# Block-sparse attention and a gated feed-forward on one core: one rank per piece of work in place of offsets by kind

## The chip, the core and the metric

The kernel runs on one core of a Trainium2 chip. A core has five engines that run side by side, each through its own program in order: TensorE (PE in the profile; its weight loads are PEld), VectorE (DVE), ScalarE (ACT), GpSimd (POOL) and SyncE (SP). They meet through semaphores. DMA transfers are issued by SP and POOL and carried by 16 DMA engines; those that SP issues form one queue (hardware_dynamic in the profile), those that POOL issues another (software_dynamic). The metric is the time of one execution on the device in microseconds (us).

## The reference

Four batches, eight heads, 768 tokens, 64 values a head. The sequence is cut into 24 blocks of 32 tokens. A query block sees its own block and both neighbours, the first and the last block, and three sampled blocks; the first and the last query block see everything. Duplicates among these count once, which is what the mask is for. The attention's output, 3072 tokens by 512, goes through a gated feed-forward.

```python
scores = scale * np.matmul(q, k.transpose(0, 1, 3, 2))
...
scores = np.where(mask, scores, -1000000000.0)
scores = scores - np.max(scores, axis=-1, keepdims=True)
attn = np.exp(scores)
attn = attn / (np.sum(attn, axis=-1, keepdims=True) + 1e-09)
return np.matmul(attn, v).astype(np.float32)
...
gate = 1.0 / (1.0 + np.exp(-(x @ w_gate)))     # 512 -> 1536
val = x @ w_val                                # 512 -> 1536
return (gate * val @ w_out).astype(np.float32) # 1536 -> 512
```

## The kernel before

**Pieces.** The kernel first describes its work as some 1,390 pieces (class `Op`). A piece is a handful of instructions on one engine, or on either of two, with an estimated duration, the pieces it depends on, the buffers it takes and gives back, and a priority `prio`. A planner (`Planner.run`) then lays all pieces out in an estimated time: at each turn it takes the engine that can start soonest, and on it, among the pieces that can start within 0.02 us of the earliest (0.2 us on TensorE), the one with the lowest priority; for a piece with two engines it takes the one that would end it first. The result is one fixed order of instructions on each engine, with buffers assigned. The planner's times are estimates and reach the chip only as that order: on the chip every engine goes through its list and waits where a semaphore makes it wait. An `after` between two pieces binds the planner alone.

**The attention of a batch b** (names as in the code, b is the first figure):

- `ldv`, `ldk`, `ldq`: loads by POOL's queue (L559, L563), float32 in HBM to float16. In batches 1 to 3 `shk`, `shq` (L722) then put K and Q by row; `vsh` (L773, VectorE) does so for V, `scr` (L782) writes these rows to a scratch in HBM, and from there the rows of a query block's window (`w`, L815, V1) and of its sampled blocks (`vg`, L894, three transfers a block, V2) are gathered; `vfl` and `vfc` (L827, L829) fill in the rows of the first and the last block. `ldq` of batch 1 to 3 is issued behind `shk`.
- `trk`, `trq` (L743, L746): K and Q are transposed on TensorE, `evk`, `evq` (L756, L761, L763) copy them to KT and QT. Batch 0 transposes Q in two parts. `kg` (L870, POOL) gathers the sampled blocks of K, `kfl` (L881) the first and the last.
- Eleven steps of two query blocks each, named after the first block: scores `sc` (L914, L921, TensorE), maximum `mx` (L930, VectorE), exponential with row sums `ex` in two halves (L942, ScalarE), reciprocal `rz` (L949), scaling `sl` in two halves (L962, L965), transposes `tp` (L976, TensorE), copy `te` (L982), product with V `pv` (L995, TensorE), copy to the feed-forward's input `xe` (L1011, L1016). In batches 2 and 3 two steps' scores form one piece. Two pairs of PSUM banks (`spool`) hold scores, two banks (`xpool`, `ptpool`) everything else of the attention.
- The first and last query block, which see all keys, go through `dsc`, `dmx`, `dex`, `dsl`, `dtp`, `dte`, `dpv`, `dxe` (L644, L1046 to L1100), one for each pair of heads.

**The feed-forward** has seven groups of tokens: groups 0 and 1 have 256 tokens, the others 512. A group has twelve slices f of the inner dimension; for each a gate piece `pg{g}_{f}` and a value piece, here written `fv{g}_{f}`, of four matmuls (both L1138), then `th` (tanh, L1146) and `h` (L1151). The outputs follow, `py{g}_{t}` (L1173, twelve matmuls), `ys` (L1180, L1182), `st` (the store by SP, L1187). A group's slices can start once all `xe` and `dxe` of its tokens are done and the slice's weights (`wg`, `wv` in four chunks of three slices, L578; `wo`, L586) have landed. Which slice comes when is open.

**Fill.** Where the plan shows TensorE idle in the first 60 us, matmuls on the identity (`fill`, L1207) are put in, 0.23 us each by the plan.

**Priorities before.** Each piece has a due time from its place in the loop (batch, step, stage); `OFFSETS` adds one number for a kind and batch (`evk1`) and one for a third or quarter of its steps (`ex0.d`). `GATES` lets chunks of the weights go after given gathers of batch 0, `LGATE` the loads of the next batch after a gather of this one. `Planner.FETCH` says how long the planner lets the fetch of 256 of TensorE's instructions take, with and without a transfer by POOL's queue under way.

## Time and profile before

| | us |
|---|---|
| times of the runs | 331.94, 333.45, 333.73 |
| median | 333.45 |
| the profiled execution's own time | 333.25 |
| its span | 331.5 |
| TensorE busy | 309.1 |
| VectorE busy | 241.4 |
| ScalarE busy | 219.1 |
| GpSimd busy | 100.9 |

The span goes from the first instruction to the last; 1.75 us of the profiled execution lie around it. The page's second part cuts the span into 40 slices of 8.29 us. A line of groups reads: line, engine, operation, what is written from what, shapes, count, then busy time, mean duration of one in ns, and the idle time before them with what ended it. Matmuls overlap in the pipeline, so a matmul's own duration is longer than its share of TensorE's time; what a piece costs TensorE is read from the starts of pieces that follow each other without a wait.

### The profile page before, as it was taken

What the parts mean: (1) busy time and instruction counts of PE and PEld (TensorE: products, weight loads), DVE (VectorE), ACT (ScalarE), POOL (GpSimd) and SP (SyncE); (2) the same over time, 40 slices, a digit from 0 to 9 for tenths busy, and PEclk for the clock granted to TensorE, in tenths of its full rate; (3) what the DMA queues carried; (4) which work ended last, traced back from release to release, by engine and by line L of the source; (5) the groups of instructions that cost most, each with busy time, mean ns of one, the idle gap of its engine ahead of it and who ended that gap; (6) DMA issues with size and microseconds to landing.
All of it is one profiled execution on the core that took longest, in us unless ns stands there. A gap on an engine that the chain in (4) does not pass through costs nothing.

```text
span 331.5 us, 12349 instructions
## 1 busy us (share of the span) xinstructions
PE 309.1 (93%) x4568; PEld 187.1 (56%) x4568; DVE 241.4 (73%) x542; ACT 219.1 (66%) x650; POOL 100.9 (30%) x332
## 2 busy tenths in 40 slices
PE   6998887998899799999999999999999999999996
PEld 2555566866766356655555655655655665444443
DVE  3399899936887979878898969999996577504310
ACT  1248889854597789766998566679995868423322
POOL 6499642036743632402330427022220010000000
PEclk9999999999999889999999999999999999999999
DMA  7959999979449862235389093531323400020002
GB/s 116 195 186 228 224 226 227 222 184 269 110 69 231 242 136 87 71 96 145 115 159 190 32 223 114 157 96 35 108 72 116 117 11 3 0 97 32 0 34 95
DMA packets 42063, 41.99 MB, mean 127 GB/s; under 512 B 6323, under 2 KB 38196, under 8 KB 42004
## 3 DMA queue, kind: packets, MB, share of 16 engines
q0 software_dynamic: 17376, 16.39, 30.0%
q1 hardware_dynamic: 24628, 24.83, 25.4%
q8 instruction: 36, 0.59, 0.8%
q14 instruction: 23, 0.19, 0.2%
HBM read 45.97 MB, written 9.44 MB: 167 GB/s over the span
## 4 chain that ended last, share of the span: by engine, by line
PE 62%; DVE 13%; DMA 9%; issue 5%; ACT 5%; SPq 3%; POOL 1%; POOLq 0%; DVEq 0%
PE bank L1138 30%; PE bank L1173 13%; DMA V<-scr 5%; PE bank L976 4%; PE bank L995 3%; ACT P L942 3%; DMA out_dram<-YS 2%; SPq L894 2%; PE twin L921 2%; DVE NM L930 2%; DVE V L827 2%; DVE HT L1151 2%; PE twin L1207 2%; DVE P L965 1%; DMA scr<-stg 1%
## 5 line engine op out<-in xcount | busy, mean ns | idle before, releaser
L942 ACT ACTIVATE P<-twin,NM 128x256 f16<-128x256 f32 x176 | 81.5, 484 | 16.0 <-DVE NM L930 15.6
L870 POOL COPY KG<-KT 128x64 f32 x264 | 51.1, 245 | 121.2 <-PE twin L921 121.0
L1138 PE MATMUL bank<-XA,wg 128*128 128x512 f16 (+1 forms) x336 | 77.0, 352 | 2.0 <-DVE HT L1151 1.1
L1138 PE MATMUL bank<-XA,wv 128*128 128x512 f16 (+1 forms) x336 | 76.3, 350 | 2.1 <-ACT TH L1146 1.0
L1151 DVE SCALAR_TENSOR_TENSOR HT<-TH,bank 128x512 f16<-128x512 f32 (+1 forms) x84 | 50.9, 608 | 33.9 <-PE bank L1138 29.4
L1173 PE MATMUL bank<-wo,HT 128*128 128x512 f16 (+1 forms) x300 | 65.0, 371 | 0.0
L1146 ACT ACTIVATE TH<-bank 128x512 f32<-128x512 f32 (+1 forms) x84 | 45.5, 543 | 27.6 <-PE bank L1138 24.8
L930 DVE TENSOR_REDUCE NM<-twin 128x4 f32<-128x1024 f32 x44 | 52.4, 1216 | 0.5 <-PE twin L921 0.2
L1138 PEld LDWEIGHTS <-wv 128*128 128x128 f16 x336 | 31.4, 98 | 28.6 <-issue 4.9
L1173 PEld LDWEIGHTS <-HT 128*128 128x128 f16 x300 | 28.5, 98 | 29.8 <-issue 0.3
L1138 PEld LDWEIGHTS <-wg 128*128 128x128 f16 x336 | 30.1, 98 | 22.9 <-issue 3.1
L942 ACT ACTIVATION_READ_ACCUMULATOR P<-twin,NM 128x1 f32 x176 | 38.0, 216 | 0.0
L965 DVE TENSOR_SCALAR P<-P,ZZ 128x256 f16<-128x256 f16 x138 | 35.6, 318 | 1.5
L995 PEld LDWEIGHTS <-V 128*128 128x128 f16 x704 | 26.0, 98 | 13.7 <-issue 6.2
L1182 ACT ACTIVATE YS<-bank 128x512 f32<-128x512 f32 (+1 forms) x16 | 9.1, 571 | 28.7 <-PE bank L1173 28.7
L976 PEld LDWEIGHTS <-P 128*128 128x128 f16 x352 | 22.3, 98 | 9.4 <-issue 1.8
L995 PE MATMUL bank<-PTS,V 128*128 128x64 f16 x528 | 22.0, 193 | 4.3 <-DVE PTS L982 1.8
L976 PE MATMUL bank<-ident,P 128*128 128x128 f16 x304 | 23.5, 219 | 0.8 <-DVE P L965 0.4
L982 DVE COPY PTS<-bank 128x1024 f16<-128x1024 f16 x23 | 15.7, 681 | 6.0 <-PE bank L976 6.0
L962 ACT ACTIVATE P<-P,ZZ 128x256 f16<-128x256 f16 x38 | 17.1, 503 | 3.0 <-DVE ZZ L949 2.9
L921 PE MATMUL twin<-KG,QT 64*32 64x160 f16 x704 | 19.0, 236 | 0.0
L982 ACT COPY PTS<-bank 128x1024 f16<-128x1024 f16 x15 | 15.2, 1010 | 5.7 <-PE bank L976 5.4
(85 smaller groups left out, 372.4 us busy)
## 6 DMA issues: line engine op xcount, KB each, us to landing
V<-scr SPq DMA_DIRECT2D x264, 32.0 KB, 3.0
out_dram<-YS SPq DMA_DIRECT2D x23, 256.0 KB, 2.1
V<-scr SPq DMA_DIRECT2D x14, 288.0 KB, 3.3
stg<-in_v_dram POOLq DMA_DIRECT2D x4, 768.0 KB, 9.1
stg<-in_k_dram POOLq DMA_DIRECT2D x3, 768.0 KB, 14.2
scr<-stg SPq DMA_DIRECT2D x3, 768.0 KB, 4.4
stg<-in_q_dram POOLq DMA_DIRECT2D x3, 768.0 KB, 7.5
V<-scr SPq DMA_DIRECT2D x6, 384.0 KB, 5.4
```

What stands on the lines that cost most here:

```text
L870: pin(nc.gpsimd.tensor_copy(t[:, :, 1 + n], KW[r][:, :, bass.ds(vals[(i - i0) * 3 + n], BLK // 2)]))
L921: pin(nc.tensor.matmul(t[hh][cs, u, c0:c1], QT[r][rs, p, BLK * i : BLK * i + BLK], src, start=False, stop=True, skip_group_check=True))
L930: pin(nc.vector.tensor_reduce(NM[o.slots[hz][1]][:, 0:4], t, axis=AX.X, op=ALU.max, negate=True))
L942: pin(nc.scalar.activation(pb[:, u, :], t[:, u, :], AF.Exp, bias=NM[z][:, x : x + 1], scale=1.0, accum_out=ZZ[z][:, x : x + 1]))
L965: pin(nc.vector.tensor_scalar(pb[:, u, :], in0=pb[:, u, :], scalar1=ZZ[z][:, 2 * hh + u : 2 * hh + u + 1], scalar2=None, op0=ALU.mult))
L976: pin(nc.tensor.transpose(t[:, c * 128 : c * 128 + 128], pb[:, c * 128 : c * 128 + 128], ident))
L982: pin(copy(o)(PTS[pl.handles[hTS][1]].rearrange("k c q -> k (c q)"), banks[o.slots[hT][1]].bitcast(f16)))
L995: pin(nc.tensor.matmul(t[:, u, p, :], vt[:, ws, p * 128 : p * 128 + 128], pt[:, u, c, :, 32 * p : 32 * p + 32], start=(c == 0), stop=(c == ...
L1138: pin(nc.tensor.matmul(t, wt[:, c, f_ * 128 : f_ * 128 + 128], XT[g][:, c, :], start=(c == 0), stop=(c == 3)))
L1146: pin(nc.scalar.activation(TH[o.slots[ht][1]][:, 0:n], banks[o.slots[hg][1]][:, 0:n], AF.Tanh, bias=0.0, scale=0.5))
L1151: pin(nc.vector.scalar_tensor_tensor(HT[:, f_, hoff : hoff + n], in0=TH[o.slots[ht][1]][:, 0:n], scalar=1.0, in1=banks[o.slots[hv][1]][:, ...
L1173: pin(nc.tensor.matmul(t, HT[:, f_, hoff + tt * 128 : hoff + tt * 128 + 128], wo[:, f_, cols], start=(f_ == 0), stop=(f_ == NF - 1)))
```

## The change

Every piece gets a rank of its own (`RANKS`, one number for each piece in the order in which the code makes them), which takes the place of its due time and offsets. The ranks, the gates and the planner's list of durations were annealed together. The instructions themselves, their shapes and their number stay as they are, but for six more matmuls of `fill` (82 for 76) and for pieces that go to the other of their two engines. `trs` makes the last transposes of K and Q, which give the buffer back, depend on the others, whose order among themselves is now open.

The planner's durations: fetch of TensorE's instructions 7.8 and 3.8 us (7.0 and 3.6), `vg` 1.65 (1.6), `evk` 0.88 and 0.76 (0.85 and 0.7), `vfc` of n units 0.06 + 0.56 n on POOL and 0.12 + 0.44 n on VectorE (0.44 n and 0.3 n), `kg` 0.58 (0.54).

```diff
-GATES = {0: 4, 2: 7, 3: 7, 4: 9, 6: 5, 7: 7, 8: 6}
-LGATE = {1: 10, 2: 11, 3: 2}
-OFFSETS = {
-    "dense1": 0.26, "dense2": 0.10, "dense3": 0.10, "evk0": -0.74, "evk1": -0.80, "evk2": -1.45, "evk3": -0.55,
...
-def kind(o):
...
-def third(o, k):
...
+GATES = {4: 5, 7: 10, 10: 10}
+LGATE = {1: 11, 2: 11, 3: 7}
+RANKS = [
+    95, 31, 147, 27, 14, 3, 1, 20, 17, 18, 13, 9, 24, 24, 0, 28, 39, 11, 71, 36, 51, 358, 33, 345, 32, 344, 41, 130,
...
+]
-    PIECE, FIRST, FETCH = 256, 150, {True: 7.0, False: 3.6}
+    PIECE, FIRST, FETCH = 256, 150, {True: 7.8, False: 3.8}
-    VGATHER = [("SP", 1.6)] * 4
+    VGATHER = [("SP", 1.65)] * 4
+            trs = []
...
-                           deps=(shs[-1:] if b else [ld[x if parts > 1 else p * len(ld) // NP]]) + [c_dma] + kq_users[b - 2],
+                           deps=(shs[-1:] if b else [ld[x if parts > 1 else p * len(ld) // NP]]) + [c_dma] + kq_users[b - 2] + (trs if p == NP - 1 and x == parts - 1 else []),
...
+                    trs.append(tr)
...
-                    res.append(P(f"ev{nm}{b}{p}{x}", ("DVE", "ACT"), (0.85, 0.7) if nm == "k" else (0.06 + 0.0044 * n, 0.17 + 0.0055 * n), f_ev, deps=[tr],
+                    res.append(P(f"ev{nm}{b}{p}{x}", ("DVE", "ACT"), (0.88, 0.76) if nm == "k" else (0.06 + 0.0044 * n, 0.17 + 0.0055 * n), f_ev, deps=[tr],
...
-                filled[x] = P(f"vfc{b}{x}", ("POOL", "DVE"), (0.06 + 0.44 * most[x], 0.12 + 0.3 * most[x]), f_fc, port=True,
+                filled[x] = P(f"vfc{b}{x}", ("POOL", "DVE"), (0.06 + 0.56 * most[x], 0.12 + 0.44 * most[x]), f_fc, port=True,
...
-                kg = P(hkg, "POOL", 0.54, f_kg, deps=[kfl[ks], held["POOL"][part][0]], prio=pr - 1,
+                kg = P(hkg, "POOL", 0.58, f_kg, deps=[kfl[ks], held["POOL"][part][0]], prio=pr - 1,
...
-    for o in pl.ops:
-        k = kind(o)
-        o.prio += OFFSETS.get(k, 0.0) + OFFSETS.get(third(o, k), 0.0)
+    for o, rank in zip(pl.ops, RANKS, strict=True):
+        o.prio = rank
```

What the planner makes of it, by the two programs (both can be built without a chip). TensorE's list has 408 pieces in both; the place of some of them, before and after:

| piece on TensorE | place before | place after |
|---|---|---|
| first slice of group 0 | 52 (`pg0_0`) | 52 (`pg0_7`) |
| `pv0_4`, `pv0_6`, `pv0_8`, `pv0_10` | 27, 32, 37, 47 | 46, 47, 48, 50 |
| `pv0_14` | 62 | 82 |
| first `trk` of batch 1 | 97 | 94 |
| first output of group 0 | 96 | 105 |
| first `trq` of batch 1 | 113 | 109 |
| first `sc` of batch 1 | 120 | 116 |
| `pv1_8`, `pv1_10` | 143, 144 | 146, 147 |
| first `trk` of batch 2 | 152 | 154 |
| first `trk` of batch 3 | 261 | 211 |
| first `sc` of batch 3 | 285 | 290 |
| first output of group 4 | 321 | 318 |
| first slice of group 6 | 379 | 379 |

Before, batch 1's first `trk` stands behind all twelve slices of group 0, one slice of group 1 and the first output of group 0; after, behind eleven slices of group 0, one slice and a gate piece of group 1, and no output. SP's list after: the gathers of batch 0 in the order 11, 9, 4, 5, 8, 10, 6, 7, 16, 12, 17, 13, then `w0_18`, 18, 15, `w0_1`, 3, 1, 2, 14, 19, `w0_20`, 21, `scr1`, 22, 20; before: 4 to 9, `w0_18`, 10 to 13, `w0_1`, 14 to 17, `w0_20`, 18, 19, 2, 3, 1, 22, `scr1`, 20, 21. POOL's list: `memset`, on which the mask waits, stands behind the six first transfers after and ahead of them before; `ldv2` and `ldk2` stand behind `kg1_18` and `kg1_19` after, behind `kg1_14` and `kg1_15` before; between `ldk2` and `shk2` stand six `kg` before and seven after; in batch 3 three `vfc` stand ahead of the `kfl` and `kg`. VectorE's list: `vsh1` at place 80 (88 before).

Pieces that change engine, as counts: `vfc` on VectorE 6 (10 before), on POOL 10 (6); `xe` on VectorE 12 (17), on ScalarE 32 (27); `evk` on VectorE 6 (4), on ScalarE 10 (12); `dte` on VectorE 12 (9), on ScalarE 4 (7); `dxe` on VectorE 6 (8), on ScalarE 10 (8); `kfl` on VectorE 6 (4), on POOL 10 (12); one of three `shq` on VectorE (0); `te`, `sl`, `evq` and `ys` one piece each.

## Prediction

> **What bounds the kernel now.** I read the page's busy times first, then the stretches, the waits, and the timelines of TensorE and GpSimd.

> ```profile
> span 331.5 us, 12349 instructions
> PE 309.1 (93%) x4568; PEld 187.1 (56%) x4568; DVE 241.4 (73%) x542; ACT 219.1 (66%) x650; POOL 100.9 (30%) x332
> ...
> DMA  7959999979449862235389093531323400020002
> ...
> PE 62%; DVE 13%; DMA 9%; issue 5%; ACT 5%; SPq 3%; POOL 1%; POOLq 0%; DVEq 0%
> ```

> TensorE is the bound over the whole, with 93%, and DMA is full up to about 83 us (slices 3 to 9). The stretches, cut where TensorE's list has its milestones, tell where TensorE isn't the bound:

> ```profile
> core 0: us, PE busy (x) PEld busy (x) DVE busy (x) ACT busy (x) POOL busy (x), PEclk, DMA share, GB/s
> 18.20:44.60 26.40, 22.43 (x494) 13.66 (x488) 24.07 (x55) 21.23 (x73) 22.71 (x62) 1.00 1.05 200
> 44.60:72.10 27.50, 23.66 (x423) 18.94 (x421) 22.42 (x62) 21.52 (x68) 5.13 (x15) 1.00 1.14 224
> 72.10:86.80 14.70, 12.44 (x157) 9.56 (x155) 10.27 (x17) 6.52 (x15) 9.24 (x20) 1.00 1.00 219
> 86.80:112.90 26.10, 22.27 (x502) 15.21 (x501) 21.86 (x46) 21.31 (x76) 11.90 (x46) 1.00 0.74 167
> 112.90:146.80 33.90, 33.76 (x485) 20.78 (x486) 29.86 (x77) 26.54 (x72) 11.62 (x34) 0.95 0.42 100
> 195.20:243.30 48.10, 47.22 (x837) 28.42 (x835) 43.60 (x91) 37.03 (x111) 13.47 (x63) 1.00 0.41 110
> ```

> In batch 0 (18.2 to 44.6) VectorE is busy 91% of the time; from 112.9 on TensorE 98% and more. Between, TensorE gets behind. The two places that matter most are the transposes of the next batch's K, which wait for its load:

> ```profile
> 69.15 1.89 POOL L722 COPY stg<-stg 96x2048 f32<-96x2048 f32 x1 [12.28 <-DMA stg<-in_k_dram]
> ...
> 95.71 0.89 POOL L559 DMA_DIRECT2D stg<-in_v_dram  x1
> 96.59 0.78 POOL L563 DMA_DIRECT2D stg<-in_k_dram  x1
> ...
> 110.95 1.89 POOL L722 COPY stg<-stg 96x2048 f32<-96x2048 f32 x1 [2.31 <-DVE PTS L982]
> ```

> ```profile
> 109.69 1.04 PE L1138 MATMUL bank<-XA,wg 128*128 128x512 f16 x4
> 112.90 0.51 PE L743 MATMUL bank<-ident,stg 96*128 96x96 f16 x8 [2.17 <-POOL stg L722]
> ```

> K of batch 1 is down at 69.1 and put in order at 71.0; K of batch 2 is issued at 96.6, down 14.2 us later (110.8), and TensorE stands 2.2 us for it.

> **The measure.** What a piece costs TensorE I read from starts of pieces that follow without a wait:

> ```profile
> 286.57 10.52 PE L1173 MATMUL bank<-wo,HT 128*128 128x512 f16 x48
> 296.93 1.03 PE L1138 MATMUL bank<-XA,wg 128*128 128x512 f16 x4
> 297.80 1.03 PE L1138 MATMUL bank<-XA,wv 128*128 128x512 f16 x4
> ```

> An output is (296.93 - 286.57) / 4 = 2.59, a slice piece 0.865 (0.44 with 256 tokens). In the same way scores 0.50, or 0.89 for two steps, `tp` 0.45, `pv` 0.47, transposes of K or Q 0.34 (0.25 for the smaller part of batch 0's Q), `dsc` 0.45, `dtp` and `dpv` 0.34. 120 and 48 slice pieces, 24 outputs, 24 and 10 scores, 44 `tp` and `pv`, 36 transposes of K and Q and 42 dense pieces make 275.2 us; none goes away. So I follow the lag, time less work done; at TensorE's end (328.2) it is 53.0, and 3.3 us of copy and store come after. The column "after" is worked out below.

> | milestone | before: time, work, lag | after |
> |---|---|---|
> | first slice | 44.6, 14.6, 30.0 | 45.4, 14.3, 31.1 |
> | first `trk`, batch 1 | 72.2, 36.6, 35.6 | 72.5, 33.1, 39.4 |
> | first `sc`, batch 1 | 86.8, 48.1, 38.8 | 86.5, 46.3, 40.2 |
> | first `trk`, batch 2 | 112.9, 68.4, 44.5 | 112.6, 69.3, 43.3 |
> | end | 328.2, 275.2, 53.0 | 325.7, 275.2, 50.5 |

> **The change, part by part.**

> *Durations of the planner, `trs`, gates:* they put no instruction on the chip; 0 by themselves. Their cover is total: TensorE's list already runs the transposes in order. The six more fills (6 x 0.23 = 1.4 us) stand before the first slice, where VectorE sets the time.

> *Start.* `memset` behind six issues of POOL (ending at 6.16) moves the mask (3.61 us on VectorE) from 2.0 to about 6.4 to 10.0; VectorE had nothing before 10.7. 0, with 0.7 us of cover; without it each us would shift batch 0. By the sums of VectorE's list the copy that the first slice waits for (`xe0_10`) comes at 31.5 us of its work instead of 30.7: +0.8, so 45.4. The slice is now f = 7, whose weights land at 44.8 in the trace of before and stand as far forward in POOL's queue as then: no further wait.

> *To batch 1's K.* TensorE now has 33.05 - 14.34 = 18.7 us to do before the first `trk`, VectorE 18.9 (31.5 to 50.4), ScalarE 19.5. `vsh1` comes earlier on VectorE and waits for V, down at 64.35, about 2 us; `pv0_14` moves behind 18 gathers (with the windows 24 portions of 96 KB, which before were down at 60.8). Walking through the list with the rows' durations I reach `trk` at 68 to 69, before K is there; that is the cover of all these stalls, some 3 us. K stands behind the same transfers as before, but `scr1` (768 KB, SP) now goes at 65.4 instead of 68.2, beside K. Loads of K took 4.7 us behind V's landing with 27% of the DMA time in SP's queue (64.4 to 69.1) and 7.4 us with 59% (103.4 to 110.8): K is late by 0 to 2.75 us. I take 1.4, the middle, as `scr1` comes in part of the time. 71.1 + 1.4 = 72.5.

> [...] The 27% and 59% agree that SP's queue takes a share when it has work. [...]

> *To batch 1's scores.* Behind the first `trk` stand 13.3 us of work (before 11.5), both outputs of group 0 among it. `shq1` now stands behind one more `vfc` (1.6 us on POOL) and is done at about 81.5, ahead of the `trq` at 83. 72.5 + 13.3 = 85.8; I add 0.7 for gaps marked "issue", of which before had 0.50 and 0.59 here. 86.5.

> *Batch 1.* ScalarE becomes the limit: from the first exponential (1.9 us behind the scores' start) to `te1_8` its list has 12 `ex` (0.90), 6 `th` (0.35), 4 `te` (0.91) and 2 `xe` (0.75), 18.0 us; two more `ex` and two `xe`, 3.3, to `xe1_10`, for which group 2's first slice waits; then 2.2 of TensorE to `trk`. 86.5 + 1.9 + 18.0 + 3.3 + 2.2 = 111.9, with handovers 112.0. If ScalarE were busy at 89%, the highest share that I saw in a stretch (11.19 of 12.6 in 32 to 44.6), it would be 2.6 more; with 0 and 2.6 as ends I take 0.6, nearer 0, since from 40.6 to 44.2 it ran without a wait where its inputs stood ready. 112.6. K of batch 2 doesn't hold it: `ldk2` goes about 95.3, behind `kg1_19`, which `sc1_14` releases at 92.5, and 14.2 + 1.9 make 111.4. So the wait of 2.2 us goes, and ScalarE is what is late next.

> *After.* The lag grew by 8.5 from here. Clock 0.95 in 112.9 to 146.8 is 1.7 of it, unchanged. Batch 3's `trk` go from place 261 to 211, `shk3` being free some 10 us earlier: 0.97 of waits (193 to 195) go. The two gaps of 0.49 and 0.72 at 210 and 222 may; I take 0.3 of them. 7.2 remains. From 112.9 on VectorE loses work (in all 8 us: four `vfc` at 1.3 to 1.8, five `xe` at 0.85, against two `evk`, three `dte`, one `shq`); ScalarE gains 1.2; worth 0, since TensorE hides both. The `vfc` on POOL ahead of batch 3's `kg` need 5 us behind `pv2_1`; 10.1 us of TensorE's work cover them, and without cover sc3 would be late.

> Sum: 3.3 + 325.7 = 329.0, that is 2.5 less than the span; 333.25 - 2.5 = 330.75 as the profiled execution. It lay 0.2 under the median: **331.0**.

> **Rivals.**

> *ScalarE stays behind (slower).* From batch 1's first exponential (88.4) to `pv1_2` ScalarE has 44.8 us of work. At the 82% that it was busy in 86.8 to 112.9 (21.31 of 26.1) it needs 54.6, and `pv1_2` comes at 143.0 with 93.9 of work done, lag 49.1, where before had 47.1 (142.8, 95.7). If nothing is saved later that is 333.45 + 2.0 = 335.5. Below 85% it is slower than before at all. For it: no stretch shows ScalarE over 90%. Against: its waits there were for VectorE, which loses work.

> *Nothing gained.* K of batch 1 at its late end (1.35 more) and ScalarE at 92% (21.3 / 0.92 is 1.85 of waits for 0.6, 1.25 more): 331.0 + 2.6 = 333.6.

> *Gaps in TensorE's own program go (more gained).* "issue" has 5% of the chain:

> ```profile
> 204.60 1.60 issue
> ...
> 221.76 1.09 issue
> ```

> With 0.40 and 0.35 beside them, 3.4 us behind 195. If these are waits for program packets and the longer allowance spreads the dense pieces, 331.0 - 3.4 = 327.6. Against: TensorE's own gaps there are 1.3 us.

> [...]

> **How the numbers follow.** A measurement here can tell 0.5%, 1.7 us, from no change: 331.8 to 335.1. Forecast (328.9 to 331.8) 0.33; gaps go 0.15; nothing gained 0.19; ScalarE 0.33, which holds other stalls of a new order too. Faster 0.48, same 0.19, slower 0.33. Range: down to the gaps' case with K on time and ScalarE without waits (327.6 - 1.4 - 0.6 = 325.6), up to ScalarE's case with K at its late end and the 0.7 of gaps once more (335.5 + 1.35 + 0.7 = 337.5).

> **What would show it.** First slice at 45 to 46; first `trk` of batch 1 at 71 to 74 behind a wait for POOL's copy, now some 3 us; first scores of batch 1 at 86 to 88; no wait of TensorE for POOL at batch 2's K; ScalarE over 90% busy in 88 to 110; TensorE's end near 325.7. Wrong if K of batch 1 lands after 73, if `trk` is reached late because gathers of batch 0 are, or if ScalarE waits in batch 1.

## The result, and the profile after

The changed kernel takes 337.92 us (median of 16 executions, 335.50 to 339.27), the kernel before 333.31 (16 executions, 331.33 to 337.05): a ratio of 1.0141, with a 95% interval of 1.0117 to 1.0165. The change makes the kernel 1.4% slower. The profiled execution took 335.5 us, the fastest of the sixteen, with a span of 333.7.

These are the parts of the changed kernel's page that answer to those shown of before: the span, the busy times, the DMA's slices, and the shares of the chain.

```profile
span 333.7 us, 12285 instructions
PE 310.8 (93%) x4574; PEld 187.6 (56%) x4574; DVE 239.2 (72%) x523; ACT 219.1 (66%) x664; POOL 104.7 (31%) x337
...
DMA  7969999979569774969340143444214120010002
...
PE 65%; ACT 11%; DVE 10%; DMA 8%; issue 3%; SPq 1%; POOL 1%; DVEq 0%; POOLq 0%
```

Nothing in them explains 4.6 us: the busy times have hardly moved. The stretches of the changed kernel do (columns: stretch, its length, busy time of each engine with the number of instructions in brackets, granted clock, DMA share, GB/s):

```profile
core 0: us, PE busy (x) PEld busy (x) DVE busy (x) ACT busy (x) POOL busy (x), PEclk, DMA share, GB/s
...
44.60:72.10 27.50, 23.18 (x450) 18.86 (x449) 23.02 (x55) 21.74 (x76) 5.99 (x20) 0.94 1.14 228
72.10:86.80 14.70, 13.60 (x174) 9.84 (x171) 11.59 (x18) 7.18 (x18) 6.61 (x17) 1.00 0.84 176
86.80:112.90 26.10, 24.55 (x534) 17.42 (x532) 22.29 (x57) 24.33 (x84) 12.73 (x49) 1.00 0.75 163
112.90:146.80 33.90, 33.90 (x491) 20.76 (x490) 29.20 (x58) 27.15 (x76) 14.84 (x35) 1.00 0.83 165
146.80:195.20 48.40, 42.54 (x609) 24.66 (x608) 35.07 (x71) 29.69 (x89) 9.27 (x38) 0.96 0.42 107
195.20:243.30 48.10, 47.45 (x794) 28.27 (x792) 40.50 (x90) 37.83 (x120) 18.15 (x66) 1.00 0.37 103
```

The one stretch of these that the prediction does not show of before:

```profile
146.80:195.20 48.40, 47.41 (x742) 27.76 (x738) 42.01 (x91) 37.99 (x120) 13.80 (x52) 1.00 0.58 135
```

Batch 1 (86.8 to 112.9) went as forecast: ScalarE is busy 24.33 of 26.1 us, 93%, where it had 82%, and TensorE waits less. TensorE is never idle in 112.9 to 146.8. The loss lies in one row: 146.8 to 195.2, where TensorE is idle for 5.9 us (before 1.0) and its clock falls to 0.96 (before 1.00). DMA has moved too: it is busy 0.83 in 112.9 to 146.8, where before it was 0.42.

Lines of the chain of work that ended last, in that stretch of the changed kernel (start, us, what), and below it the timelines of SP, VectorE and TensorE (start, us, what, and in brackets the idle time before and what ended it):

```profile
146.68 2.59 PE bank L1199 x12
149.27 4.53 DMA V<-scr
153.87 6.00 DMA out_dram<-YS
163.77 2.72 PE bank L1164 x8
```

```profile
146.87 2.30 SPq L920 DMA_DIRECT2D V<-scr  x5
149.27 0.88 SPq L841 DMA_DIRECT2D V<-scr  x2
150.40 3.06 SPq L920 DMA_DIRECT2D V<-scr  x6
153.87 0.38 SPq L1213 DMA_DIRECT2D out_dram<-YS  x1
```

```profile
150.53 2.36 DVE L956 TENSOR_REDUCE NM<-twin 128x4 f32<-128x1024 f32 x2 [0.25 <-PE twin L947]
159.96 0.69 DVE L1206 TENSOR_SCALAR YS<-bank 128x512 f32<-128x512 f32 x1 [7.07 <-DMA out_dram<-YS]
160.57 0.58 DVE L1126 CAST XA<-bank 64x32 f16<-64x32 f32 x4
161.18 0.18 DVE L975 RECIPROCAL ZZ<-ZZ 128x4 f32<-128x4 f32 x1
161.40 0.88 DVE L991 TENSOR_SCALAR P<-P,ZZ 128x256 f16<-128x256 f16 x4
162.19 0.17 DVE L975 RECIPROCAL ZZ<-ZZ 128x4 f32<-128x4 f32 x1
162.39 0.48 DVE L991 TENSOR_SCALAR P<-P,ZZ 128x256 f16<-128x256 f16 x2
```

```profile
162.74 1.04 PE L1002 MATMUL bank<-ident,P 128*128 128x128 f16 x8 [5.02 <-DVE P L991]
163.56 1.91 PE L1164 MATMUL bank<-XA,wg 128*128 128x512 f16 x4
```

This is one stall, and the four views show it from end to end. There are three output buffers, `YS`. The planner gave `ys2_3_0`, the fourth output tile's copy of group 2, the buffer of `ys2_0_0`, since by its estimate the store of that one, `st2_0_0`, was down 2.7 us before the copy starts (149.7 for 152.4); another buffer stood free. On the chip `ys2_0_0` is copied by 146.65. SP issues its store only at 153.87, behind two windows (`w2_11`, `w2_15`, L841) and gathers (L920): it is busy issuing these until 153.46, and what the chain names last is the landing of `w2_11`, 0.3 us later (149.27 and 4.53 us). The store lands 6.0 us after its issue, at 159.9. VectorE stands still for 7.07 us at the copy. Behind it in VectorE's list stand `dxe13` and the reciprocals and scalings `rz2` and `sl2` of two attention steps, whose inputs are there by 155.6. So ScalarE gets no work (idle 156.2 to 162.4), and TensorE waits 5.02 us for the transposes `tp2_12`. In the kernel before the copy `ys2_1_0` waits 0.28 us for the same store, and TensorE does not notice:

```profile
155.17 0.69 DVE L1180 TENSOR_SCALAR YS<-bank 128x512 f32<-128x512 f32 x1 [0.28 <-DMA out_dram<-YS]
```

The lags (time less TensorE work done, in us) of the profiled executions, beside the forecast; the last column is the experiment `e5_store_ahead` below:

| milestone | before | forecast | changed kernel | store ahead |
|---|---|---|---|---|
| first slice | 30.0 | 31.1 | 32.2 (at 46.5) | 31.3 |
| first `trk`, batch 1 | 35.6 | 39.4 | 39.0 (72.1) | 38.1 |
| first `sc`, batch 1 | 38.8 | 40.2 | 40.7 (87.0) | 41.1 |
| first `trk`, batch 2 | 44.5 | 43.3 | 44.0 (113.3) | 44.4 |
| first output of group 2 | 47.4 | | 44.6 (143.3) | 45.0 |
| first `tp2` of 157 to 163 | 47.6 | | 49.9 (162.7) | 45.2 |
| TensorE's end | 53.0 | 50.5 | 55.2 (330.5) | 49.2 |

At the first output of group 2 the changed kernel is 2.8 us ahead of before; 20 us later it is 2.3 behind. Where a loss of TensorE is given below without a line of the profile, it is taken from starts in the same way: the start of a piece, less the start of the piece before it and what that one costs. This is up to 0.2 us more than the idle time in the brackets, and it counts as well what half clock costs, that is, a stretch with a granted clock of 0.50.

### The profile page after: what moved, and what is told of

Same layout as the page of the kernel before. It is cut to its first block, busy times and chain, and to the rows that moved or that the text cites. A ratio compares the mean times of both kernels' runs of the same rounds, so it can differ in the third digit from the quotient of the medians.

```text
span 333.7 us, 12285 instructions
## 1 busy us (share of the span) xinstructions
PE 310.8 (93%) x4574; PEld 187.6 (56%) x4574; DVE 239.2 (72%) x523; ACT 219.1 (66%) x664; POOL 104.7 (31%) x337
## 4 chain that ended last, share of the span: by engine, by line
PE 65%; ACT 11%; DVE 10%; DMA 8%; issue 3%; SPq 1%; POOL 1%; DVEq 0%; POOLq 0%
PE bank L1164 31%; PE bank L1199 14%; ACT P L968 6%; DMA stg<-in_q_dram 4%; PE bank L1021 3%; PE bank L1002 3%; PE twin L947 2%; DVE V L853 2%; DMA out_dram<-YS 2%; DMA FL<-scr 1%; ACT PTS L1008 1%; DMA V<-scr 1%; PE twin L1021 1%; DVE NM L1072 1%; PE twin L1002 1%
## 5 line engine op out<-in xcount | busy, mean ns | idle before, releaser
L968 ACT ACTIVATE P<-twin,NM 128x256 f16<-128x256 f32 x176 | 81.5, 486 | 17.3 <-DVE NM L956 16.2
L896 POOL COPY KG<-KT 128x64 f32 x264 | 50.6, 243 | 117.9 <-PE twin L947 112.4
L1164 PE MATMUL bank<-XA,wv 128*128 128x512 f16 (+1 forms) x332 | 75.5, 352 | 0.0
L1177 DVE SCALAR_TENSOR_TENSOR HT<-TH,bank 128x512 f16<-128x512 f32 (+1 forms) x83 | 50.1, 607 | 33.1 <-PE bank L1164 29.7
L1002 PE MATMUL bank<-ident,P 128*128 128x128 f16 x264 | 20.7, 222 | 8.9 <-DVE P L991 6.3
L855 POOL COPY V<-FL 32x768 f32<-32x768 f32 (+1 forms) x20 | 18.3, 944 | 18.9 <-PE bank L1021 15.7
L988 ACT ACTIVATE P<-P,ZZ 128x256 f16<-128x256 f16 x36 | 16.4, 508 | 8.7 <-DVE ZZ L975 8.7
L1021 PE MATMUL bank<-PTS,V 128*128 128x64 f16 x464 | 19.0, 195 | 0.3 <-DVE XA L1037 0.2
L947 PE MATMUL twin<-KG,QT 64*32 64x160 f16 x704 | 18.7, 235 | 0.0
L1037 ACT CAST XA<-bank 64x256 f16<-64x256 f32 x38 | 13.9, 366 | 5.2 <-PE bank L1021 4.8
## 6 DMA issues: line engine op xcount, KB each, us to landing
stg<-in_k_dram POOLq DMA_DIRECT2D x3, 768.0 KB, 14.3
```

The source lines that it names most:

```text
L855: pin(nc.gpsimd.tensor_copy(dst.bitcast(f32), src.bitcast(f32).broadcast_to([BLK, n, DM // 2])))
L896: pin(nc.gpsimd.tensor_copy(t[:, :, 1 + n], KW[r][:, :, bass.ds(vals[(i - i0) * 3 + n], BLK // 2)]))
L947: pin(nc.tensor.matmul(t[hh][cs, u, c0:c1], QT[r][rs, p, BLK * i : BLK * i + BLK], src, start=False, stop=True, skip_group_check=True))
L968: pin(nc.scalar.activation(pb[:, u, :], t[:, u, :], AF.Exp, bias=NM[z][:, x : x + 1], scale=1.0, accum_out=ZZ[z][:, x : x + 1]))
L1002: pin(nc.tensor.transpose(t[:, c * 128 : c * 128 + 128], pb[:, c * 128 : c * 128 + 128], ident))
L1021: pin(nc.tensor.matmul(t[:, u, p, :], vt[:, ws, p * 128 : p * 128 + 128], pt[:, u, c, :, 32 * p : 32 * p + 32], start=(c == 0), stop=(c == ...
```

## The experiments

All but one (`e7_fetch_back`) add lines behind `order = pl.run()`, so that the plan is the same but for what is named. `behind(p, a, b)` stands for "move a and b directly behind p in the order in which the instructions are emitted":

```python
def behind(place, *names):
    moved = [next(o for o in order if o.name == x) for x in names]
    for o in moved:
        order.remove(o)
    at = next(x for x, o in enumerate(order) if o.name == place) + 1
    order[at:at] = moved
```

**Another buffer.** In the first three only the choice among the output buffers differs.

```diff
+    for o in order:
+        for h, y in (("ys2_3_0", 2), ("ys2_1_0", 0)):
+            if h in o.slots:
+                o.slots[h] = ("ys", y)
```

> Theory (one output buffer): in the changed kernel VectorE stands from 152.9 to 160.0 at ys2_3, because its buffer is that of ys2_0, whose store goes at 153.9 and lands at 159.9; TensorE loses 5.1 us at tp2_12 and some 1.2 more just behind. With the free third buffer for ys2_3 (and that of ys2_0 for ys2_1) the order stays and the wait goes: 5 to 6 us less than the changed kernel, about 332 us against 333.3 before, ratio 0.995; TensorE's wait ahead of tp2_12 under 0.5 us. Rival (gathers and DMA late): the softmax of batch 2 waits for rows of V anyway, so TensorE waits further on: at least 336, ratio 1.008 or more. Second rival (clock): the lower granted clock of this order, 0.98 to 0.99, is the cost: 337, ratio 1.012, whatever the buffer.

Measured: 333.10 us (330.86 to 336.01, 12 executions) against 333.31 of before in the same series, ratio 1.0025 (0.9984 to 1.0066). `tp2_12` starts at 157.6 with no wait, and TensorE's end has lag 50.6. The stall goes with the buffer; 4.8 us of the median come back. But the median only equals that of before. Its own waits show why: now `ys2_1_0` uses the buffer of the late store.

```profile
DVE YS L1206 <- DMA out_dram<-YS: 3.0, 1, 3.0
```

The columns are engine and line, what it waited for, us in total, times, and the longest. It is one wait of 3.0 us on VectorE, until 159.4. TensorE loses 1.18 before `fv3_6`, which by the profile waits for the bank that this copy empties, and 0.69 before `fv3_2`, which waits for a piece `h` that stands behind the copy on VectorE.

All outputs in turn, in the changed kernel and in the kernel before:

```diff
+    turn_of = {}
+    for o in order:
+        for h in o.slots:
+            if h.startswith("ys"):
+                o.slots[h] = ("ys", turn_of.setdefault(h, len(turn_of)) % 3)
```

> All output tiles take the three buffers in turn. Buffer theory: as with the one exchange, 331 to 332.5 us, ratio 0.993 to 0.998, since only group 2 waited for a store; up to 1 us less if later groups waited a little too. Rival (gathers, clock): 336 to 338.

> The same turns in the kernel before. Buffer theory: there three copies waited about 1 us each for a store (155.2, 157.5, 161.6) and TensorE lost at most 0.5 near them: 332.5 to 333.5, ratio 0.997 to 1.000. Rival (the buffers are what ails both orders): 330 or less.

Measured: changed kernel in turn 332.93 (331.27 to 336.07), ratio 1.0015 (0.9975 to 1.0055), lag at the end 51.9; before in turn 332.57 (330.35 to 335.04), ratio 0.998 (0.9944 to 1.0016), lag 53.8. In turn, `ys2_1_0` gets the late store's buffer in the changed kernel as well; it starts at 160.7, 0.1 behind the landing, and TensorE loses 1.38 and 0.69. The first is a little above the 331 to 332.5 expected; before gains nothing that can be told from zero. So the buffer rule as such isn't what matters: what matters is a copy that meets this store.

**The store itself.** A first try moved `st2_0_0` directly behind `ys2_0_0`:

```diff
+    first = next(o for o in order if o.name == "st2_0_0")
+    order.remove(first)
+    order.insert(next(x for x, o in enumerate(order) if o.name == "ys2_0_0") + 1, first)
```

> The buffers stay as planned, but SP issues st2_0 directly behind its copy's place, ahead of w2_11, w2_15 and two gathers. If SP's order makes the store late, it lands by 153.5 and all of the 5 to 6 us come back, 332. If the DMA traffic ahead of it makes it late (3 to 6 us from issue to landing), it lands near 153 to 155 and 3 to 5 us come back, 333 to 335. Rival (gathers, clock): 337.

Measured: 337.05 (331.53 to 338.40, 6 executions); store issued at 153.73, down at 160.32, `tp2_12` at 163.2. This missed its aim: no piece of SP stands between `ys2_0_0` and `st2_0_0` in the order, so the lists of all five engines are as they were, and these are six more executions of the changed kernel. Five took 336.77 to 338.40; one took 331.53, and as its trace was not kept, why is open. What holds the store stands ahead of both. The next one moves that away.

```diff
+    behind("st2_0_0", "vg2_5", "w2_11", "w2_15", "vg2_16", "vg2_14")
```

> The changed kernel with its buffers as they are; SP issues the store of the first output of group 2 (st2_0_0) directly behind vg2_9, ahead of vg2_5, w2_11, w2_15, vg2_16 and vg2_14. Theory A (the store is late because SP comes to it late): it is issued at about 148 instead of 153.9, down by 151.5, and VectorE copies ys2_3_0 at 153 as soon as TensorE has the output. The 5.1 us wait of TensorE at 157.7 goes, and with it the two smaller waits of 1.18 and 0.69 that the kernel with exchanged buffers still had at 158 to 163, which were for the same store. Profiled end of TensorE 324 to 326, median 331 to 333. Theory B (the store is late because the DMA queues are full of batch 3's loads, which the new order issues some 35 us sooner): it needs 6 us from issue to landing wherever it stands, is down at 154, VectorE waits 1 us, and the time is that of the kernel with exchanged buffers, 333.

Measured: **329.70** (328.16 to 330.93, 6 executions) against 333.51 (17 executions), ratio 0.9885 (0.9846 to 0.9923). With one store moved past five of SP's pieces the new order is 1.2% faster than before, and below the 331 to 333 expected. SP, then TensorE, of this kernel:

```profile
147.83 0.38 SPq L1213 DMA_DIRECT2D out_dram<-YS  x1
148.40 1.31 SPq L920 DMA_DIRECT2D V<-scr  x3
```

```profile
158.04 0.62 PE L1002 MATMUL bank<-ident,P 128*128 128x128 f16 x8
158.50 1.03 PE L1164 MATMUL bank<-XA,wg 128*128 128x512 f16 x4
159.37 1.03 PE L1164 MATMUL bank<-XA,wv 128*128 128x512 f16 x4
```

The store is issued 6.0 us sooner, is down after 2.1 us (149.94), and the waits of TensorE before `tp2_12`, `fv3_6` and `fv3_2` are gone. Theory A holds for SP's place. That the store now needs 2.1 instead of 6.0 us to land says that theory B has a part as well: DMA is busy 0.49 in 147.8 to 150.0 here, and 1.05 in 153.87 to 159.86 in the changed kernel.

> The changed kernel, with the load of batch 3's Q (ldq30) issued by GpSimd behind the K blocks kg2_11, at about 158 instead of 149. SP's order and the buffers are as in the changed kernel. Theory A: the store still goes at about 153.9, behind the windows and gathers of batch 2 that SP issues ahead of it, and lands at 157 to 160; VectorE waits 4 to 7 us, and the median is 336 to 338. Theory B: without this load in the queues the store is down 2 to 2.5 us behind its issue, at 156.3; VectorE waits 3.4 us instead of 7.1, TensorE 1 to 2 instead of 5.1, and the median is about 334.5.

```diff
+    behind("kg2_11", "ldq30")
```

Measured: 336.51 (335.46 to 342.50, 8 executions), ratio 1.0094 (1.0060 to 1.0127). With batch 3's load of Q out of the way the same store, issued at 154.11, is down at 157.69, after 3.6 us and not the 6.0 to 7.2 of six profiles with this load beside it; VectorE waits 4.05 us instead of 7.07 and TensorE 2.1 instead of 5.0. So the transfers that the new order brings forward do lengthen the store's way, by 2.4 us against the changed kernel, as theory B has it. The time gains little. In the profiled execution, 2.1 us above the median, Q of batch 3 is now late: it lands at 168.64, VectorE copies it (`shq3`, and `evk320` behind it), TensorE loses 3.5 us before `trq320` (170.87), and the half clock of 169.96 to 176.79 takes more. Both causes add up: SP comes to the store 6 us later than it can, and the store then takes 4 us more than it does at 148.

**The same stall put into the kernel before.**

```diff
+    behind("vg2_12", "st2_0_0")
```

> The kernel before, with the same thing put into it: SP issues the store st2_0_0 behind w2_15 and vg2_12, at about 156.3 instead of 150.8; ys2_1_0 uses the same buffer (0), as in the kernel before. If one copy that waits at the head of VectorE's queue is what cost the changed kernel its time, VectorE stands still from 154.2 until the store is down at 158 to 160.5 (instead of 155.1), ScalarE and TensorE follow it, and the median rises by 3 to 5 us, to 336 to 338. If the loss belonged to the new order as a whole and the wait only stood beside it, VectorE's slack takes up such a wait, and the median stays within 1 us of 333.4.

Measured: 336.36 (335.90 to 339.38, 4 executions) against 332.36 (16 executions), ratio 1.0133 (1.0074 to 1.0193). VectorE of this kernel:

```profile
152.18 1.81 DVE L827 COPY V<-FL 32x1536 f16<-32x1536 f16 x2
157.94 0.69 DVE L1180 TENSOR_SCALAR YS<-bank 128x512 f32<-128x512 f32 x1 [3.95 <-DMA out_dram<-YS]
```

One store, issued 4.8 us later (155.62 for 150.83), makes VectorE wait 3.95 us for 0.28. TensorE waits 2.5 before `tp2_4`, and the half clock of 159.35 to 162.77 costs it 1.4 more before `pv2_4`. The old order loses 4.0 us of the median, nearly the 4.6 of the whole change.

**What stands behind the copy.** Here the copy still waits, but last:

```diff
+    behind("sl2_12_0", "ys2_3_0")
```

> The changed kernel with SP's order and the buffers as they are, and ys2_3_0 moved five places back in VectorE's list, behind sl2_12_0. It still waits for the store (down at about 159.9), but dxe13, rz2_14, sl2_14, rz2_12 and sl2_12 no longer stand behind it. If the loss is what stands behind the copy, tp2_12 starts at 158 instead of 162.7; then pg3_6, which needs the bank that ys2_3_0 empties, waits until 160.7, so of 5.1 us about 2 remain, and the median is 334 to 336. If the bank were what TensorE really waits for, the time stays at 337 to 338.

Measured: 340.08 (339.31 to 343.81, 4 executions), ratio 1.0253 (1.0189 to 1.0317). In this kernel the tile's own store `st2_3_0` stands ahead of its copy, so that one output tile is stored from what the buffer held before and is wrong, and the copy has that store to wait for as well: it comes at 165.9, and `pg3_6`, which needs the bank, stood still for 8 us. Its median therefore says nothing about the question. The first half of the expectation can be read all the same: `tp2_12` started at 158.1, lag 45.3, without a wait. The same with the store moved along:

```diff
+    behind("sl2_12_0", "ys2_3_0", "st2_3_0")
```

> The changed kernel with SP's place for st2_0_0 and the buffers as they are, and ys2_3_0 and its own store st2_3_0 moved behind sl2_12_0 in the lists of VectorE and SP. If the loss is what stands behind the copy on VectorE, tp2_12 starts at 158 (lag 45.3) although the copy still comes only when the store is down, at about 160; then pg3_6, which needs the bank that ys2_3_0 empties, waits until 161, 2 of the 5.1 us, and the median is 334 to 336. If that bank is what the time hangs on, the wait only moves from tp2_12 to pg3_6, the lag at pg3_6 stays at 50 or more, and the median is 337 to 338.

Measured: 335.28 (331.93 to 336.82, 10 executions), ratio 1.0052 (1.0012 to 1.0092), within the 334 to 336 expected. This series ran on another chip, with before at 333.63 (13 executions); by the ratios to before it is 3.0 us better than the changed kernel. VectorE:

```profile
158.24 0.48 DVE L991 TENSOR_SCALAR P<-P,ZZ 128x256 f16<-128x256 f16 x2
159.87 1.29 DVE L1206 TENSOR_SCALAR YS<-bank 128x512 f32<-128x512 f32 x2 [1.15 <-DMA out_dram<-YS]
```

The store lands when it did (159.85), and VectorE waits 1.15 us for it instead of 7.07. In the profiled execution, the fastest of the ten, TensorE loses nothing at `tp2_12`; but it had come to batch 2 late, with lag 46.4, since K of batch 1 landed at 70.25, and that covered the store. By the ratios 3.0 of the 8.5 us between the changed kernel and the one with the store ahead (1.0141, 1.0052 and 0.9885) hang on the pieces behind the copy. The other 5.6 would be the copy itself, through the bank that `pg3_6` needs, as expected in kind; no profile of a middling execution shows it, so that part is argued.

**A part undone, and more moves.**

```diff
-    PIECE, FIRST, FETCH = 256, 150, {True: 7.8, False: 3.8}
+    PIECE, FIRST, FETCH = 256, 150, {True: 7.0, False: 3.6}
```

> One part of the change undone: the planner's allowance for TensorE's program packets is 7.0 and 3.6 again; the ranks and the other durations are the new ones. The planner then gives ys2_3_0 the third buffer and ys2_1_0 (on ScalarE) the first, and 112 pieces of TensorE's list stand elsewhere than in the changed kernel. Theory A: the loss of the changed kernel is the one copy that waits for the store, so this kernel has no wait of over 2 us at 155 to 163, and its time is that of the kernels whose buffers were exchanged, 331.5 to 334.5. Rival: the new ranks make an order that is slower in itself, or the longer allowance is what the new order needs; then TensorE's lag is already larger than 45.5 at batch 2's first transposes of K, or its own gaps marked as issue grow by over 1 us behind 195, and the time stays at 336 or above.

Measured: 351.22 (350.47 to 352.78, 4 executions), ratio 1.0525 (1.0479 to 1.0572). TensorE has no wait of over 0.5 us at 155 to 163, and yet it is the slowest of all: the rival's outcome. The sign that the rival named is there, a lag of 46.4 at batch 2's `trk`, but most of the loss comes later: the lag is 47.5 at 160 and 72.5 at the end. Six losses of TensorE of 0.9 to 1.4 us in a row at 207 to 218, the later ones at half clock (211.98 to 222.22), and more at 260 to 272, stand between the steps of one batch's attention. In the first of these stretches TensorE has 184.0 us of work behind it when batch 3's scores start (changed kernel 170.2, before 164.4), so little is left to put between the steps. The 1,387 ranks fit one list of durations: with another list they give another order, which nobody has tuned. So the parts of this change can't be priced one by one, and what the longer allowance alone is worth stays open.

```diff
+    behind("st2_0_0", "vg2_5", "w2_11", "w2_15", "vg2_16", "vg2_14")
+    behind("kg1_6", "shq1")
+    behind("evq130", "vfc12")
+    behind("sl0_2_1", "sl0_2_0")
```

> The store ahead as in e5_store_ahead, and three moves in batch 0 and 1 at waits of TensorE that the profile of the changed kernel shows: the copy shq1 on GpSimd ahead of vfc13; VectorE's vfc12 behind evq130; VectorE's sl0_2_0 directly behind sl0_2_1, so that it does not run beside GpSimd's shk1 (it took 1.99 us there, against 0.48 for others of its kind). The waits of TensorE before tp0_2 (1.27) and before trq110 (1.22) should go or fall below 0.4. If TensorE's lag at batch 2's first transposes of K falls by the same 2 us, to about 42, the median is 2 us below that of e5_store_ahead, 329 to 331. If ScalarE, 93% busy in batch 1, takes the gain back, that lag stays at 43.5 to 44 and the time is that of e5_store_ahead, 331 to 333.

Measured: 329.62 (328.24 to 331.72, 9 executions), ratio 0.9888 (0.9853 to 0.9924), the time of `e5_store_ahead`. The waits before `tp0_2` and `trq110` are gone; but they are not in `e5_store_ahead` either, where TensorE comes to batch 1 earlier and waits 2.2 us for K's copy, so the moves can claim only the 1.0 us that is lost there before `trq120` and not here. With it the first scores of batch 1 come with lag 40.1 instead of 41.1; at batch 2's `trk` it is 44.5 against 44.4. Between these two milestones the lag grows by 3.3 in nine other profiles of this order, here by 4.4: `vfc12`, moved behind `evq130`, takes 1.3 us on VectorE just ahead of `mx1_4`, and ScalarE's first exponential comes 1.1 us later behind the scores (3.0 for 1.9). The gain was given back there by one of the three moves.

> The kernel with the store ahead (e5_store_ahead), and six fill matmuls of 0.23 us (1.4 us in all) ahead of trk100, where TensorE waits 2.2 us for GpSimd's copy of K. All profiles so far show the granted clock in stretches of 3.41 us, and each stretch in which TensorE was busy for under half of the time is followed by one at half clock (nine such pairs; stretches with 54% or more are not). With the fill the stretch at 68 is busy 0.8 instead of 0.40, so the one after it stays at full clock. If that half clock costs what it takes away, 1.7 us of TensorE at most, the lag at batch 1's scores falls from 41.1 to about 40 and the median is 0.5 to 1.5 us below 329.7. If ScalarE takes it back in batch 1, the clock is 1.00 there and the median stays at 329.2 to 330.2.

```diff
+    behind("st2_0_0", "vg2_5", "w2_11", "w2_15", "vg2_16", "vg2_14")
+    at = next(x for x, o in enumerate(order) if o.name == "trk100")
+    bank = order[at].slots["trk100"][1]
+    def f_wait(o):
+        for x in range(6):
+            pin(nc.tensor.matmul(banks[bank].rearrange("p (x n) -> p x n", n=128), ident, ident.unsqueeze(1).broadcast_to([128, 4, 128]),
+                                 start=True, stop=True, skip_group_check=True))
+    order.insert(at, Op("fillk", "PE", 0.0, f_wait, count=6))
```

Measured: 330.77 (328.61 to 333.47, 12 executions), ratio 0.9941 (0.9906 to 0.9976). The two stretches at K of batch 1, first without the fill (`e5_store_ahead`), then with it:

```profile
67.92:71.33 3.41, 1.36 (x20) 1.04 (x19) 1.43 (x4) 0.50 (x2) 2.14 (x2) 1.00 0.78 262
71.33:74.74 3.41, 3.41 (x28) 2.68 (x26) 0.42 (x1) 1.98 (x3) 0.48 (x1) 0.50 0.72 77
```

```profile
66.97:70.38 3.41, 3.05 (x26) 1.96 (x24) 2.00 (x6) 1.28 (x3) 0.97 (x1) 1.00 0.98 313
70.38:73.80 3.42, 2.44 (x39) 2.30 (x40) 0.42 (x1) 1.87 (x3) 1.64 (x2) 1.00 0.41 57
```

With TensorE busy for 3.05 us instead of 1.36 the clock behind stays at 1.00, and the profiled execution has lag 40.1 at the scores and 48.3 at the end, 0.9 less than without the fill. The median shows no such gain: 0.9941 of before against 0.9885 without the fill, with intervals that overlap. Five of its twelve executions, those with a mean clock of 0.999 or more, took 328.6 to 330.1, the seven others 330.7 to 333.5. Where their clock fell isn't recorded, so the effect is shown for one execution; what it is worth over all of them is not.

## Why the prediction was wrong

The forecast was 331.0 us, with a range up to 337.5; it came out as 337.92.

**The step that failed** is the paragraph "After", and in it the sentence that VectorE's change from 112.9 on is "worth 0, since TensorE hides both". It sums VectorE's work over a stretch of 215 us and does not walk through its list. (The sum was off too: from 112.9 on VectorE's busy time fell by 3.3 us, 155.5 to 152.1, and not by 8.) The lag was to grow by 7.2 from batch 2's `trk` to the end; it grew by 11.2. One wait of 5.02 us and the half clock behind it (TensorE busy 2.92 us at clock 0.50 in 162.24 to 165.65, so 1.5 us of work lost) make 6.5. With the store ahead the growth is 4.8, and 11.2 less 4.8 is 6.4. By the medians the stall costs 8.2 us (337.92 less 329.70); the traced execution was the fastest of its sixteen, and where the others lose the rest no trace shows. The trace of before had the three lines that this step needed: a copy by VectorE that waits for `out_dram<-YS`, a store that SP issues only behind gathers, and transfers of batch 3 that the change moves forward by 36 us (`ldv3` and `ldk3` from 167 to 131). The plan of the changed kernel shows the shared buffer and the five pieces ahead of the store. The prediction listed places on TensorE and POOL, and of SP's list only batch 0.

**Start.** Forecast 45.4 with lag 31.1, measured 46.5. The profiled execution ran a half-clock stretch at 18.9; the seven profiles of this order that have none there show 45.3 to 46.0, lag 31.0 to 31.6. Right but for that stretch. The cover of the mask was larger than written: only its last four instructions wait for `memset` (1.64 us), and it ends at 7.0, not at 10.0.

**Batch 1's K.** The 1.4 us for `scr1` beside it were not there: K landed at 68.97, with `scr1` issued at 66.4. In ten profiles of this order (not counting `e7_fetch_back`) it landed at 68.9 to 69.4, but for one at 70.25; in three of the old order at 69.0 to 69.9. That K comes late when SP's queue takes a larger share of the DMA time was an estimate from two loads of before, and it did not show: in 64.4 to 69.0 SP's queue had 59.8% of the DMA time (before 25.8%), and the moved bytes rose from 181 to 292 GB/s, so K paid nothing. The milestone came right, 72.1 for 72.5, by luck: TensorE itself arrived there 3 us late, through the late start, a half-clock stretch at 56.4 and a loss of 1.40 before `tp0_2` (the 1.33 before `tp0_16` is in all ten profiles). Where it arrived earlier, as with the store ahead, it waited for K's copy until 71.1.

**Batch 1.** ScalarE as the limit, at 93%, with the wait for K of batch 2 gone: right. `trk` came at 113.3 for 112.6. The rival "ScalarE stays behind" is refuted by the row of 86.8 to 112.9.

**Clock.** The 1.7 us of half clock at 114 in before were held unchanged. They go with the wait: none of the profiles of the new order (`e7_fetch_back` apart) has a half-clock stretch there, and of the old order the two with a wait of 2.2 us at batch 2's `trk` have one, the third (`e9_before_late`, 1.0 us) has none. With the store ahead this is 1.7 of the 2.4 us by which the growth of the lag, 4.8, is below the 7.2 forecast. The other 0.7 is not taken apart.

**The sum.** With the one stall taken out it is 329.7 us: 3.8 below before, where 2.5 were forecast. So the direction that the prediction had worked out holds without the stall, though not each term: K's 1.4 us was not there, and the 1.7 us of clock went. It gave 0.33 to the slower side, for ScalarE and "other stalls of a new order too"; it was one of the latter. That the upper end of the range, worked out for ScalarE, comes within 0.5 us of the measured time is luck.

## What to carry to other kernels

A new order of the same work is to be read engine by engine for one pattern: a piece that waits for a DMA, with work behind it that other engines need. Its price isn't in any sum of busy times. For each buffer that is used again, find the transfer that must be down, where its issue stands on its queue, and what else is in flight then; a planner that estimates a store as done will hand out a buffer that is not free while a free one lies beside it. And where a plan is tuned together with its durations, put one thing right in the plan that came out rather than change a duration back: the first gave 2.4%, the second cost 4%.

## What the runs showed of the hardware

```profile
158.83:162.24 3.41, 0.00 (x0) 0.00 (x0) 2.20 (x11) 0.00 (x0) 1.08 (x7) 1.00 0.65 249
162.24:165.65 3.41, 2.92 (x13) 1.48 (x14) 3.34 (x7) 2.05 (x4) 0.00 (x0) 0.50 0.24 45
```

So in these profiles a wait cost itself, and up to 1.7 us more (an estimate, half of 3.41) for the stretch at half clock if it filled over half of one at full clock; one of 2 us did or didn't, by where it fell (2.05 us of idle time in `e5_store_ahead` at 69.1 did, 2.08 in `e6_later_q` at 158.6 did not). In five profiles two or three stretches at half clock followed in a row, from 163.45 to 170.28 in `e11_copy_behind`.

**Pieces of VectorE took longer beside GpSimd's copies.** In the changed kernel two scalings took 0.48 us just before GpSimd put K in order, and two others 2.12 beside it:

```profile
68.29 0.48 DVE L991 TENSOR_SCALAR P<-P,ZZ 128x256 f16<-128x256 f16 x2
68.80 0.42 DVE L1177 SCALAR_TENSOR_TENSOR HT<-TH,bank 128x256 f16<-128x256 f32 x1
69.14 2.12 DVE L991 TENSOR_SCALAR P<-P,ZZ 128x256 f16<-128x256 f16 x2
```

```profile
69.09 1.89 POOL L744 COPY stg<-stg 96x2048 f32<-96x2048 f32 x1 [11.24 <-DMA stg<-in_k_dram]
```

In the same way `vfc10` took 3.5 us beside `vfc13` and `shq1` (80 to 83), and 1.4 in the five profiles in which the next of these two began 0.8 us or more behind it. `sl0_2_0`, the piece of these two scalings, and `vfc10` stand on VectorE ahead of what TensorE waited for at `tp0_2` and `trq110` (1.40 and 1.22), two waits that no step of the prediction had. Why they took longer no run shows; the two scalings end 0.3 us behind the copy (71.26 and 70.98).

**A 256 KB store took from 2.0 to 8.7 us to land**, by what else was under way: 2.1 is the median of all stores of a profile, and `st2_0_0` took 2.1 at 148 (`e5_store_ahead`, DMA busy 0.49), 3.6 at 154 without the load of Q (`e6_later_q`) and 6.0 with it (changed kernel, DMA busy 1.05); the longest of the changed kernel took 7.5 (issued at 113.7), and the longest of this order's profiles is `st1_0_0` at 114 in `e11_copy_behind`, with the 8.7.
